# Soft-MoE kernel on one core: second expert product in four column groups, weight loads at the end of attention in a listed order

## The chip, the cores and the metric

One core of one Trainium2 chip runs the whole program. The metric is device time in microseconds (us). Runs of the kernel before: 588.32, 585.62 and 587.15 us, median 587.15. The profiled execution took 587.28 us; the trace spans 585.0 us of it, so 2.3 us lie around the trace.

## The reference, cut to what matters

Three layers, all in float32. The change lies in the second and in the way from the first to it.

```python
x = attention(q, k, v, cap)            # batch 4, 12 heads, 448 rows, 64 each -> [1792, 768]
logits = x @ phi                       # [1792, 32]: 8 experts with 4 slots each
d = softmax(logits, axis=0)            # over the tokens
slot_input = (d.T @ x).reshape(8, 4, 768)
for e in range(8):
    h = np.maximum(slot_input[e] @ w1[e], 0.0)     # w1[e] is [768, 1024]
    slot_out[e] = h @ w2[e]                        # w2[e] is [1024, 768]
x = softmax(logits, axis=1) @ slot_out.reshape(32, 768)
out = mlp(x, w_in, w_out, alpha)       # 768 -> 2048 -> 768
```

The expert weights are 8 x 6 MB. They are read once; each is multiplied with a few rows only.

## The kernel before, in words

**Attention** (`attention`, L243) runs over 24 pairs of heads, four chunks of keys a pair, in the order `CHUNKS = (0, 3, 1, 2)` (L53). `qk` makes a chunk's scores and their exponentials `p`; two steps later `pv` multiplies them with the values (`o`), GpSimd adds `p` of the chunks into `acc`, and `row_sums` multiplies `acc` with `hot` (`rs`); for the last pair also `p` of its last two chunks (`rs<-p`).

**Attention's room.** Attention's SBUF pools lie one after another (L248 to L263). Bytes per partition, counted from the first: `nat0` 0 to 4096, `nat1` to 8192, `stk0` to 15872, `vn0` to 17664, `acc0` to 21248, `stk1` to 28928, the four buffers of `pt` (a full chunk's `p`, 3584 bytes each) to 32512, 36096, 39680 and 43264, the two of `ptt` (chunk 3) to 46848, `vn1` to 48640, `acc1` to 52224, then constants, `xn` and others. Even pairs use `nat0`, `stk0`, `vn0`, `acc0`, odd ones the others. The framework deals the four `pt` buffers in a fixed round: first, fourth, third, second. In the compiled program of before the last full chunks therefore lie so: pair 22's chunk 2 in the first buffer, pair 23's chunk 0 in the fourth, its chunk 1 in the third, its chunk 2 in the second.

**Weights.** `loads` (a list made ahead of time) names every weight load in the order of its use: for each expert two halves of w1 and two of w2, 1.5 MB each; the first half of `w_out` stands before expert 7. `load_next` (L130) takes the next into the first free slot. All these transfers are issued by SyncE (SP), whose instructions run in order: one that waits holds up all behind it. Ten loads go into ten slots of their own during attention. The eleventh slot holds the conversion buffer `cvbuf` of `w_in` until its last converted piece is stored to a scratch tensor in HBM (`store_w_in`, L714, SP); that function then issues the eleventh load (two transfers, L172). Seven more slots (`xtra`, 12288 bytes each) lie over attention's room from byte 0. `load_free` at L1351 fills them, by `load_part` (L119): 3072-byte pieces of a w2 half (384 KB, four of them), 4096-byte pieces of a w1 half (512 KB, three). `in_turn` (L98) keeps all of these in one order. A piece waits for the last use of every attention tile that it overlaps. Later loads wait for slots that the experts give back (`done_with`).

**Experts** (`experts`, L858). For each expert: `h`, 6 steps of K in four column groups of 256 that run side by side in the array's column quarters (L869); ReLU on ScalarE (L880); two transposes (L885); a copy by VectorE (L886); then `y` (L893), 8 steps of K in three column groups of 256:

```python
yacc[32 * g:32 * g + 32, :256],
hT[:, kk % 2, kk // 2, :],
wv[kk % 4][:, 256 * g:256 * g + 256],
```

Each float32 product stands in the trace as two records, so a step of `y` has six. `y` accumulates over all experts. The slots' rows of `h` and `y` are 32 partitions.

**After the experts**, `gather` (L907) copies `y` out of PSUM (`ysb`), turns it with two transposes (`yt`), and copies it to `so`; `mlp` follows with `aps` (L930), which reads the first `w_in` load. `warm` products (L812) fill short waits of TensorE.

Of the kernel before, what the change touches and what calls it, by code (L numbers as in the profile page):

```python
# [8 lines left out]
F32 = mybir.dt.float32  # L9
# [15 lines left out]
def tile_attention_soft_moe_mlp(ctx, tc, q, k, v, cap, phi, w1, w2, w_in, w_out, alpha, out):  # L25
    nc = tc.nc
# [24 lines left out]
    LAG = 2  # L51

    CHUNKS = (0, 3, 1, 2)  # L53
    LOADS = (4, 6, 8, 10, 12, 14, 16, 18, 19, 20, 21, 22)

    EH = 5
# [37 lines left out]
    nload = [0]  # L94
    issued = [None]
    half = []

    def in_turn(ins):  # L98
        if xslots:
            if issued[0] is not None:  # L100
                tc.add_manual_dep(ins.ins, issued[0].ins.name, NOSYNC, reason="loads in the order of their use")
            issued[0] = ins

    def may_load():
        if nload[0] == len(loads):
# [13 lines left out]
    def load_part(kind, e, i, c, t, after=None):  # L119
        if kind == "w2":  # L120
            src = w2_rows(e, i)[:, c // 2, c % 2]
        else:
            src = w1_rows(e, i)[:, c]
        ins = nc.sync.dma_start(out=t, in_=src)
        in_turn(ins)
        if after is not None:
            tc.add_manual_dep(ins.ins, after.ins.name, NOSYNC, reason="prefetch pace")
        return t

    def load_next(after=None):  # L130
        slot_no = may_load()
        free.remove(slot_no)
        kind, e, i = loads[nload[0]]
        nload[0] += 1
        if slot_no >= NA:

            ts = where.setdefault((kind, e, i), [])
            n = 3 if kind == "w1" else 4
            for c in range(len(ts), n):
                t = xslots[0].tile([128, SLOT // n], F32, tag=f"slot{slot_no}_{c}", name="w")  # L140
                ts.append(load_part(kind, e, i, c, t))
            return
        if kind == "w1":
            t = slot(slot_no, [128, 3, FE])
            src = w1_rows(e, i)
        elif kind == "w2":
            t = slot(slot_no, [128, 4, DM])
            src = w2_rows(e, i)
        elif kind == "wi":
            t = slot(slot_no, [128, KD, 512])  # L150
            src = w_in32[i].rearrange("(k p) f -> p k f", p=128)
        else:
            t = slot(slot_no, [128, 2, DM, 2], U32)
            src = w_out[256 * i:256 * i + 256].rearrange("(k p) f t -> p k f t", p=128)
        if kind == "w1":
            parts = [(t, src)]
        elif kind == "w2":
            parts = [(t[:, 2 * j:2 * j + 2], src[:, j]) for j in range(2)]
        else:
            parts = [(t[:, c], src[:, c]) for c in range(t.shape[1])]  # L160
        if kind == "wo" and i == 0:

            half.append(parts.pop())
        elif kind == "wi" and i == 0:
            parts = [
                (t[:, ks, fs], src[:, ks, fs])
                for fs in (slice(0, 256), slice(256, 512))
                for ks in (slice(0, 3), slice(3, 6))
            ]
            parts[2:2] = half  # L170
        for dst, part in parts:
            ins = nc.sync.dma_start(out=dst, in_=part)  # L172
            in_turn(ins)
            if after is not None:
                tc.add_manual_dep(ins.ins, after.ins.name, NOSYNC, reason="prefetch pace")
        if kind == "w1":
            t = [t[:, c] for c in range(3)]
        elif kind == "w2":
            t = [t[:, c] for c in range(4)]
        where[kind, e, i] = t  # L180
        held[kind, e, i] = slot_no
# [61 lines left out]
    def attention():  # L243
        with ExitStack() as pools:
            def pool(name, bufs=1, **kw):
                return pools.enter_context(tc.tile_pool(name=name, bufs=bufs, **kw))
# [4 lines left out]
            v_0 = pool("vn0")  # L251
            acc_0 = pool("acc0")
            stk_1 = pool("stk1")
            pt_p = pool("pt", 4)
            ptt_p = pool("ptt", 2)
            v_1 = pool("vn1")
# [9 lines left out]
            ps_o = pool("ps_o", space=PSUM)  # L266

            nat_p, stk_p, v_p, acc_p = (nat_0, nat_1), (stk_0, stk_1), (v_0, v_1), (acc_0, acc_1)
            stackI = ac_p.tile([128, 128], F32, name="stackI")
            sel = ac0_p.tile([128, GP, 2, 2, 64], F32R, name="sel")  # L270
            hot = ac0_p.tile([128, 64], F32, name="hot")
# [441 lines left out]

            def store_w_in(i):  # L714
                fb, kk = divmod(i, KD)
                nc.sync.dma_start(out=w_in32[fb, kk * 128:(kk + 1) * 128, :], in_=cout.pop(i))
                load_w_in(i + 2)
                if i == ncv - 1:
                    free.append(NA - 1)
                    load_next()  # L720

            def run_bg():
                while bg and min(bg) <= now[0]:
# [78 lines left out]
    def tail():  # L802
# [50 lines left out]
                )  # L853
            nc.vector.tensor_copy(out=cstk[:, b * S:(b + 1) * S], in_=ps)

        G3 = DM // 256

        def experts(which, small, ps_w, yacc, cstk=None):  # L858
            for e in which:
                if e == E - 1:  # L860
                    to_single(0)
                    split_wo(0)
                hT = small[:, 0:256].rearrange("p (u j s) -> p u j s", u=2, j=4)
                nc.gpsimd.memset(hT, 0.0)
                h1 = ps_w.tile([128, 512], F32, tag="w", name="h1")[:, :256]
                for kk in range(KD):
                    wv = where["w1", e, kk // 3]
                    for j in range(4):
                        nc.tensor.matmul(  # L869
                            h1[32 * j:32 * j + 32, :],  # L870
                            slotT[:, kk, :],
                            wv[kk % 3][:, 256 * j:256 * j + 256],
                            start=(kk == 0),
                            stop=(kk == KD - 1),
                            tile_position=(0, 32 * j),
                        )
                done_with("w1", e, 0)
                done_with("w1", e, 1)
                rl = small[:, 256:512]
                nc.scalar.activation(  # L880
                    out=rl.rearrange("q (u p) -> q p u", u=2), in_=h1.rearrange("q (p u) -> q p u", u=2), func=AF.Relu
                )
                tp = ps_w.tile([128, 512], F32, tag="w", name="tp")[:, :256]
                for u in range(2):
                    nc.tensor.transpose(tp[:, 128 * u:128 * u + 128], rl[:, 128 * u:128 * u + 128], ident)  # L885
                nc.vector.tensor_copy(  # L886
                    out=hT[:, :, :, SPE * e:SPE * e + SPE],
                    in_=tp.rearrange("p (u j s) -> p u j s", u=2, j=4)[:, :, :, SPE * e:SPE * e + SPE],
                )
                for kk in range(KE):  # L890
                    wv = where["w2", e, kk // 4]
                    for g in range(G3):
                        pe[0] = nc.tensor.matmul(  # L893
                            yacc[32 * g:32 * g + 32, :256],
                            hT[:, kk % 2, kk // 2, :],
                            wv[kk % 4][:, 256 * g:256 * g + 256],
                            start=(e == 0 and kk == 0),
                            stop=(e == E - 1 and kk == KE - 1),
                            tile_position=(0, 32 * g),
                        )  # L900
                done_with("w2", e, 0)
                done_with("w2", e, 1)
                if EH <= e < EH + B // 2:
                    for b in (2 * (e - EH), 2 * (e - EH) + 1):
                        build_c(b, ps_w, cstk)

        def gather(ps_w, yacc, so):  # L907
            warm = ps_c.tile([128, 512], F32, tag="c", name="warm")
            idle(2, warm)
            ysb = unit(7, F32, "ysb")[:32 * G3, :256]  # L910
            nc.vector.tensor_copy(out=ysb, in_=yacc[:32 * G3, :256])
            yt = ps_w.tile([128, 512], F32, tag="w", name="yt")[:, :64 * G3]
            for u in range(2):
                pe[0] = nc.tensor.transpose(
                    yt[:, 32 * G3 * u:32 * G3 * (u + 1)], ysb[:, 128 * u:128 * u + 128], ident[:32 * G3, :32 * G3]
                )
            idle(3, warm)
            for r in range(2):
                dst = so[:, :, r, :].rearrange("p (g u) s -> p u g s", u=2)
                src = yt.rearrange("p (u g s) -> p u g s", u=2, g=G3)  # L920
                nc.vector.tensor_copy(out=dst, in_=src)

        def mlp(ps_w, ps_c, so, cstk, a_stk, gr, gs, ob, more):
# [415 lines left out]
        with (  # L1339
# [4 lines left out]
            with (  # L1344
# [3 lines left out]
                small = ex2_p.tile([128, 512], F32, name="small")  # L1348
                xslots.append(xt_p)
                free.extend(range(NA, NA + NX))  # L1350
                load_free()  # L1351
                experts(range(EH), small, ps_w, yacc)
            with (
                tc.tile_pool(name="r2", bufs=1, reuse_waits="tile") as r2_p,
# [48 lines left out]
```

## Time and profile before

| what | us |
|---|---|
| median of three runs | 587.15 |
| profiled execution | 587.28 |
| span of its trace | 585.0 |
| TensorE busy | 553.1 (95% of the span) |
| VectorE busy | 435.1 (74%) |
| ScalarE busy | 377.6 (65%) |
| share of the chain that ended last: TensorE, DMA | 71%, 14% |
| of which: load of expert weights | 9% |

How to read it: attention lasts to about 261 us, the experts to 327 us, the MLP from there to the end. TensorE is busy nearly always, but a stage can still be held by something else: in the page's 40 slices (14.6 us each) the transfers move 347 to 419 GB/s in slices 17 to 25 (234 to 366 us), which hold the experts' stage, and 53 GB/s in slice 16, just ahead. The chain of waits tells which of the two ended last.

### The profile page before, as it was taken

The numbers are of one execution on the slowest core, as the hardware profiler recorded it, in microseconds if no ns is written. First come the engines' busy times: TensorE is split into PE (matmuls) and PEld (weight loads), VectorE is DVE, ScalarE is ACT, GpSimd is POOL, SyncE is SP. The second block draws the span as 40 slices with busy tenths as digits, with TensorE's granted clock in tenths as the row PEclk, the third lists the DMA queues.
The fourth block names the chain that finished last, engine by engine and source line by source line (L and its number), as shares of the span: only waits on it lengthen the run. The fifth ranks groups of instructions, "written<-read, shape, count | busy, mean of one in ns | idle before, by whom it ended". The sixth has DMA issues, their size and how long they took to land.

```text
span 585.0 us, 10832 instructions
## 1 busy us (share of the span) xinstructions
PE 553.1 (95%) x4030; PEld 384.7 (66%) x4030; DVE 435.1 (74%) x834; ACT 377.6 (65%) x617; POOL 173.9 (30%) x158
## 2 busy tenths in 40 slices
PE   5999999999999999998888799999999999999996
PEld 4444444445444545464445577878888999999996
DVE  3878777796999768460023489999999979797974
ACT  3999999898889788530011266854777755555551
POOL 0789788676785755500000000000000000000000
PEclk9999999999999999999999999999999999999999
DMA  7668789987787971999999999200120101010101
GB/s 174 155 141 251 230 263 269 266 255 200 225 256 214 326 229 53 350 347 418 416 417 419 390 404 414 111 1 1 55 55 1 55 1 54 2 55 0 55 2 54
DMA packets 83460, 110.92 MB, mean 190 GB/s; under 512 B 55376, under 2 KB 63312, under 8 KB 81872
## 3 DMA queue, kind: packets, MB, share of 16 engines
q1 hardware_dynamic: 81168, 109.28, 55.3%
q10 hardware_dynamic: 2240, 0.95, 0.6%
q8 instruction: 32, 0.52, 0.4%
q14 instruction: 20, 0.16, 0.1%
HBM read 98.41 MB, written 11.80 MB: 188 GB/s over the span
## 4 chain that ended last, share of the span: by engine, by line
PE 71%; DMA 14%; ACT 8%; DVE 5%; issue 2%; SPq 1%; ACTq 0%
PE o L295 10%; DMA w<-in_moe_w_dram 9%; PE s L295 8%; PE P L1229 7%; PE P L1227 7%; PE P L1228 7%; PE oc L1002 6%; PE oc L1008 6%; PE oc L1009 6%; DMA v<-in_v_dram 3%; ACT p L398 2%; PE aps L930 2%; ACT p L397 2%; PE nx L295 2%; PE rs L295 2%
## 5 line engine op out<-in xcount | busy, mean ns | idle before, releaser
L295 PE MATMUL o<-p,v 128*64 128x448 f32 (+1 forms) x384 | 93.3, 564 | 5.8 <-ACT xu L423 3.7
L397 ACT ACTIVATE p<-s 128x896 f32<-128x896 f32 x96 | 78.7, 821 | 21.1 <-PE s L295 18.0
L398 ACT ACTIVATE p<-p,cap 128x896 f32<-128x896 f32 x96 | 90.9, 949 | 2.3
L414 POOL TENSOR_TENSOR acc<-p 128x448 f32<-128x448 f32 x48 | 62.1, 1313 | 55.6 <-ACT p L398 55.6
L1008 PE MATMUL oc<-wsp,gr 128*128 128x512 f32 (+1 forms) x192 | 65.3, 341 | 0.0
L1009 PE MATMUL oc<-wsp,gr 128*128 128x512 f32 (+1 forms) x192 | 64.1, 337 | 0.0
L1002 PE MATMUL oc<-wsp,gr 128*128 128x512 f32 (+1 forms) x192 | 62.6, 343 | 0.0
L295 PEld LDWEIGHTS s<-qh,kh 64*128 64x128 f32 (+1 forms) x168 | 18.1, 185 | 66.5 <-issue 25.6
L1218 ACT ACTIVATE gr<-gs 128x384 fp32r<-128x384 f32 (+1 forms) x64 | 36.7, 576 | 32.8 <-DVE gs L1202 26.9
L417 POOL TENSOR_TENSOR acc<-acc,p 64x448 f32<-64x448 f32 x46 | 55.4, 1204 | 1.7
L421 POOL TENSOR_TENSOR acc<-acc,p 128x448 f32<-128x448 f32 x46 | 53.5, 1183 | 1.8
L1219 DVE TENSOR_TENSOR gr<-gs,gr 128x384 fp32r<-128x384 f32 x64 | 39.2, 620 | 17.4 <-ACT gr L1218 17.4
L295 PE MATMUL s<-qh,kh 64*128 64x448 f32 (+1 forms) x168 | 45.8, 473 | 0.0
L1227 PE MATMUL P<-wsp,gr 128*128 128x384 f32 x128 | 42.9, 335 | 0.0
L1229 PE MATMUL P<-wsp,gr 128*128 128x384 f32 x128 | 42.8, 334 | 0.0
L1228 PE MATMUL P<-wsp,gr 128*128 128x384 f32 x128 | 42.8, 334 | 0.0
L1002 PEld LDWEIGHTS oc<-wsp,gr 128*128 128x128 f32 x192 | 36.6, 192 | 5.6 <-ACT wsp L837 0.8
L1008 PEld LDWEIGHTS oc<-wsp,gr 128*128 128x128 f32 x192 | 36.8, 191 | 5.2 <-DVE wx L205 0.4
L1009 PEld LDWEIGHTS oc<-wsp,gr 128*128 128x128 f32 x192 | 36.3, 189 | 4.4 <-issue 0.4
L295 PEld LDWEIGHTS o<-p,v 128*64 128x64 f32 (+1 forms) x384 | 19.0, 134 | 30.3 <-ACT xu L423 12.3
L295 PE MATMUL s<-ql,kh 64*128 64x448 f32 (+1 forms) x168 | 35.5, 366 | 1.0 <-DVE ql L377 1.0
L295 PE MATMUL s<-qh,kl 64*128 64x448 f32 (+1 forms) x168 | 35.5, 365 | 0.0
(237 smaller groups left out, 1227.3 us busy)
## 6 DMA issues: line engine op xcount, KB each, us to landing
w<-in_moe_w_dram SPq DMA_DIRECT2D x26, 768.0 KB, 12.4
w<-in_moe_w_dram SPq DMA_DIRECT2D x12, 1536.0 KB, 12.2
cvbuf<-in_moe_w_in_dram SPq DMA_DIRECT2D x24, 512.0 KB, 5.4
w<-in_moe_w_out_dram SPq DMA_DIRECT2D x16, 768.0 KB, 11.1
w_in<-cvbuf SPq DMA_DIRECT2D x24, 256.0 KB, 2.8
w<-in_moe_w_dram SPq DMA_DIRECT2D x12, 512.0 KB, 7.4
q<-in_q_dram SPq DMA_DIRECT2D x44, 112.0 KB, 3.6
k<-in_k_dram SPq DMA_DIRECT2D x48, 96.0 KB, 4.8
```

Source lines behind the costliest of these rows:

```text
L295: ins = nc.tensor.matmul(*a, **kw)
L397: nc.scalar.activation(out=pe, in_=ps[:, :n, :S], func=AF.Tanh)
L398: nc.scalar.activation(out=pe, in_=pe, func=AF.Exp, scale=cap_sb)
L414: nc.gpsimd.tensor_add(out=a[:, u, :], in0=pt[i, 0][:, u, :], in1=pe[:, u, :])
L417: nc.gpsimd.tensor_add(out=a[r, u, :], in0=a[r, u, :], in1=pt[i, JK][r, 0, :])
L421: nc.gpsimd.tensor_add(out=a[:, u, :], in0=a[:, u, :], in1=pe[:, u, :])
L1002: ins = nc.tensor.matmul(o, gh[:, ts], wo_h[f][:, cols], start=(f == 0 and not second), stop=False)
L1008: nc.tensor.matmul(o, gh[:, ts], wo_l[f][:, cols], start=False, stop=False)
L1009: nc.tensor.matmul(o, gl[:, ts], wo_h[f][:, cols], start=False, stop=(f == KF - 1 and not more))
L1227: nc.tensor.matmul(o, hi[:, i], bh, start=(p == 0), stop=False)
L1228: nc.tensor.matmul(o, hi[:, i], bl, start=False, stop=False)
L1229: nc.tensor.matmul(o, lo[:, i], bh, start=False, stop=(p == 7))
```

## The change

- `y` takes four column groups of 192 in place of three of 256. A group's 192 columns are three runs of 64 that stand 256 apart in the weight row. A step has eight records in place of six.
- `gather` copies 128 x 192 in place of 96 x 256; six products with parts of the identity (64 columns each, in the two column halves) take the place of the two transposes; the copies to `so` keep their size.
- The last w2 half of expert 7 is read by three transfers (768, 384, 384 KB) in place of two of 768 KB.
- `store_w_in` no longer issues the eleventh load. `load_free` collects the transfers of that load and of the seven slots, and they are issued in the order `FIRST`, the others behind. They are numbered: 0 and 1 the eleventh load; 2 to 5 the first `xtra` slot (bytes 0 to 12288); 6, 7, 8 the second (to 24576); 9, 10, 11 the third (to 36864); 12 to 15 the fourth (to 49152); 16 to 19 the fifth; 20 to 25 the last two. Before, their order is 0 to 25.
- The last store of `w_in` is put behind transfers 2 and 3.
- A pool `edge` of 256 bytes stands between `stk1` and `pt`: the `pt` buffers then end at 32768, 36352, 39936 and 43520. So piece 10 (28672 to 32768) meets the first buffer alone, piece 12 (36864 to 39936) the third alone, 13 the fourth, 11 the second and third, 14 the fourth and `ptt`. Without the 256 bytes, piece 10 also meets 256 bytes of the second, and 12 of the fourth.

```diff
+    FIRST = [2, 3, 4, 5, 0, 1, 6, 12, 7, 8, 9, 13, 14, 10]
...
+    def transfer(dst, src, after=None):
+        if collected:
+            collected.append((dst, src))
+            return
+        ins = nc.sync.dma_start(out=dst, in_=src)
+        in_turn(ins)
...
+            if e == E - 1 and i == 1:
+                parts[1:] = [(t[:, 2 + u], src[:, 1, u]) for u in range(2)]
...
             stk_1 = pool("stk1")
+            edge = pool("edge")
             pt_p = pool("pt", 4)
...
                 if i == ncv - 1:
                     free.append(NA - 1)
-                    load_next()
...
-        G3 = DM // 256
+        G4 = DM // 192
...
-                    for g in range(G3):
+                    cols = wv[kk % 4].rearrange("p (u g c) -> p g u c", u=3, g=G4)
+                    for g in range(G4):
                         pe[0] = nc.tensor.matmul(
-                            yacc[32 * g:32 * g + 32, :256],
+                            yacc[32 * g:32 * g + 32, :192],
                             hT[:, kk % 2, kk // 2, :],
-                            wv[kk % 4][:, 256 * g:256 * g + 256],
+                            cols[:, g],
...
+            odd = ident.rearrange("p (k r s) -> p r k s", r=2, s=32)
+            for u in range(3):
+                for r in range(2):
+                    pe[0] = nc.tensor.matmul(
+                        yt[64 * r:64 * r + 64, 64 * u:64 * u + 64], ysb[:, 64 * u:64 * u + 64], odd[:, r],
+                        start=True, stop=True, tile_position=(0, 64 * r),
+                    )
...
+                collected.append(None)
                 load_free()
+                todo = collected[1:]
+                collected.clear()
+                first = FIRST
+                for n in first + [n for n in range(len(todo)) if n not in first]:
+                    transfer(*todo[n])
+                    if n == first[1]:
+                        tc.add_manual_dep(
+                            last_store[0].ins, issued[0].ins.name, NOSYNC, reason="room that is free sooner"
+                        )
```

## Rows read from the trace of the kernel before

**Rows 1.** Chain of waits, experts' stage: start us, us, what

```profile
271.02 17.63 DMA w<-in_moe_w_dram
...
307.39 18.76 DMA w<-in_moe_w_dram
...
326.20 1.06 PE y L893 x12
```

**Rows 2.** Timeline of TensorE, experts: start us, us, [idle before <-releaser]

```profile
261.64 2.80 PE L869 MATMUL h<-w,slotT 128*32 128x256 f32 x48
...
284.97 2.94 PE L869 MATMUL h<-w,slotT 128*32 128x256 f32 x45
...
289.49 3.44 PE L893 MATMUL y<-w,small 128*32 128x256 f32 x45 [0.35 <-DVE small L886]
...
324.24 1.06 PE L893 MATMUL y<-w,small 128*32 128x256 f32 x12 [0.23 <-DMA w<-in_moe_w_dram]
326.20 1.06 PE L893 MATMUL y<-w,small 128*32 128x256 f32 x12 [0.90 <-DMA w<-in_moe_w_dram]
```

**Rows 3.** Stretches: us, PE PEld DVE ACT POOL busy, PEclk, DMA share, GB/s

```profile
231.00:234.00 3.00, 3.00 (x38) 1.42 (x34) 2.51 (x5) 2.85 (x4) 1.38 (x1) 1.00 0.21 64
...
241.00:244.00 3.00, 2.95 (x24) 1.03 (x22) 0.38 (x1) 2.87 (x4) 0.62 (x1) 1.00 1.04 418
...
249.50:251.30 1.80, 1.80 (x20) 1.00 (x16) 1.76 (x2) 1.27 (x3) 0.00 (x0) 1.00 0.27 55
...
271.00:290.00 19.00, 16.29 (x227) 8.44 (x222) 0.58 (x3) 1.83 (x3) 0.62 (x2) 1.00 1.02 419
```

**Rows 4.** Timeline of SP's DMA issues around attention's end: start us, us

```profile
233.09 0.33 SPq L716 DMA_DIRECT2D w_in<-cvbuf  x1
...
235.17 0.81 SPq L172 DMA_DIRECT2D w<-in_moe_w_dram  x2
...
240.43 0.33 SPq L124 DMA_DIRECT2D w<-in_moe_w_dram  x1
...
243.66 1.28 SPq L124 DMA_DIRECT2D w<-in_moe_w_dram  x3
...
250.05 0.33 SPq L124 DMA_DIRECT2D w<-in_moe_w_dram  x1
...
264.23 0.33 SPq L124 DMA_DIRECT2D w<-in_moe_w_dram  x1
```

**Rows 5.** The issue at 250.05 us: KB, us from issue to landing

```profile
w<-in_moe_w_dram SPq DMA_DIRECT2D x1, 512.0 KB, 3.8
```

**Rows 6.** Timelines of TensorE and GpSimd: last uses of the `pt` buffers

```profile
239.42 0.97 PE L295 MATMUL o<-p,v 128*64 128x448 f32 x4
...
245.70 0.97 PE L295 MATMUL o<-p,v 128*64 128x448 f32 x4
...
249.00 0.97 PE L295 MATMUL o<-p,v 128*64 128x448 f32 x4
...
243.38 2.28 POOL L414 TENSOR_TENSOR acc<-p 128x448 f32<-128x448 f32 x2 [3.57 <-ACT p L398]
```

**Rows 7.** Chain of waits: four column groups of 128 columns, 6 steps of eight records

```profile
256.82 1.51 PE ss L295 x48
```

**Rows 8.** Timelines of VectorE and TensorE: `gather`

```profile
327.32 0.42 DVE L911 COPY ysb<-y 96x256 f32<-96x256 f32 x1 [5.29 <-PE y L893]
...
327.79 0.39 PE L914 MATMUL yt<-ident,ysb 96*128 96x96 f32 x2
```

**Rows 9.** Two stretches (columns as in rows 3), and the chain inside and behind the second

```profile
331.00:334.70 3.70, 1.73 (x12) 1.19 (x10) 2.92 (x7) 1.65 (x4) 0.00 (x0) 1.00 1.03 404
...
335.50:338.90 3.40, 3.40 (x20) 2.69 (x16) 3.34 (x7) 2.63 (x6) 0.00 (x0) 0.50 1.06 394
...
338.05 0.43 PE oc L1002
...
339.19 0.23 PE oc L1008
```

More of the change, by code (lines that the diff above doesn't have):

```diff
@@ L96, in tile_attention_soft_moe_mlp @@
     half = []
+    collected, last_store = [], []
     def in_turn(ins):
@@ L102, in in_turn @@
             issued[0] = ins
+    def transfer(dst, src, after=None):
[4 more added lines that the diff above has]
+        in_turn(ins)
+        if after is not None:
+            tc.add_manual_dep(ins.ins, after.ins.name, NOSYNC, reason="prefetch pace")
     def may_load():
@@ L123, in load_part @@
             src = w1_rows(e, i)[:, c]
[L124 to L127, printed above, removed]
+        transfer(t, src, after)
         return t
@@ L171, in load_next @@
         for dst, part in parts:
[L172 to L175, printed above, removed]
+            transfer(dst, part, after)
         if kind == "w1":
@@ L268, in attention @@
             nat_p, stk_p, v_p, acc_p = (nat_0, nat_1), (stk_0, stk_1), (v_0, v_1), (acc_0, acc_1)
+            edge.tile([128, 64], F32, name="edge")
             stackI = ac_p.tile([128, 128], F32, name="stackI")
@@ L715, in store_w_in @@
                 fb, kk = divmod(i, KD)
-                nc.sync.dma_start(out=w_in32[fb, kk * 128:(kk + 1) * 128, :], in_=cout.pop(i))
+                last_store[:] = [nc.sync.dma_start(out=w_in32[fb, kk * 128:(kk + 1) * 128, :], in_=cout.pop(i))]
                 load_w_in(i + 2)
@@ L909, in gather @@
             idle(2, warm)
[L910 to L916, printed above, removed]
+            ysb = unit(7, F32, "ysb")[:, :192]
+            nc.vector.tensor_copy(out=ysb, in_=yacc[:, :192])
+            yt = ps_w.tile([128, 512], F32, tag="w", name="yt")[:, :192]
+            odd = ident.rearrange("p (k r s) -> p r k s", r=2, s=32)
[5 more added lines that the diff above has]
+                    )
             idle(3, warm)
             for r in range(2):
-                dst = so[:, :, r, :].rearrange("p (g u) s -> p u g s", u=2)
-                src = yt.rearrange("p (u g s) -> p u g s", u=2, g=G3)
+                dst = so[:, :, r, :]
+                src = yt.rearrange("p (k s) -> p k s", s=32)
                 nc.vector.tensor_copy(out=dst, in_=src)
```

## The prediction, made before the changed kernel was run

> **What bounds the kernel now.** I read the chain of waits first. Through the experts it is made of weight loads, the last of them issued at 307.39 and landed at 326.15, and then one piece of `y` [rows 1]. TensorE's own timeline shows that it is nearly level with them: it works from 261.64 and waits for loads only at the end, 0.23 and 0.90 us [rows 2]. So two things of nearly equal length end this stage at 327.26: TensorE's 64.5 us of expert work, and a stream of loads. Taking 6.9 us off the first alone could show only about 1 us, for the stream ends at 326.15 whatever TensorE does.
>
> The stretches say when the stream can be shortened: not inside (418 and 419 GB/s, in 384 KB pieces and in larger ones alike), but where it stands: before 236 (64 GB/s between 231 and 234) and from 249.5 to 251.3 (55 GB/s) [rows 3]. SP's issues tell why: the eleventh load goes out at 235.17, behind the store at 233.09; pieces 6 (240.43), 7 (243.66), 10 (250.05) and 25 (264.23) wait for room [rows 4].
>
> **The change part by part.**
>
> *`y` in four groups.* From the two rows of `y`, 45 records in 3.44 and 12 in 1.06, a step of six records takes (3.44 - 1.06) / 5.5 = 0.433 us, and a start and end add 0.19 [rows 2]. With 192 columns a group in place of 256 the step becomes 0.325 if it goes by a group's columns. More records could bound it: eight in four groups have gone by in 1.51 / 6 = 0.25 [rows 7], below 0.325, so I take 0.325. What runs of 64 columns cost is shown nowhere: between nothing and a doubled step (a rival). Saved: 64 steps x 0.108 = 6.9 us of TensorE, 57.6 left, which would end at 319.3. The loads are later, so on the path this is worth only the last step's part, below.
>
> *The head of the stream.* Pieces 2 and 3 lie over `nat0` and `nat1`, which the transposes of pair 23 release near 228; they can go out behind pair 23's values at about 231. The store at 233.09 then stands behind two issues of some 0.4 us each, and its data behind 768 KB, 1.9 us; what waits for it is the eleventh load (pieces 0 and 1), and 4 and 5 (1.9 us of transfer) cover that. An issue into an empty stream lands 3.8 us later with 512 KB [rows 5], of which 1.25 are transfer at 418 GB/s and 2.5 fixed. Piece 6 waits for the `o` products of pair 22's last chunk, to 240.39 [rows 6], as now. So at that point the new stream has done all of 0 to 6 by about 244, and the old one was some 3 us behind.
>
> *The listed order.* Behind 6 comes 12. It meets the third `pt` buffer, which by the dealing of before holds pair 23's chunk 1: GpSimd reads it to 243.38 + 2.28 = 245.66, and the `o` products to 245.70 + 0.97 = 246.67 [rows 6]. So SP stands from about 241 to 246.75. Queued behind are 7, 8 and 9 (free at 243.66 now [rows 4]), 13, 14 and 10 (by the padding clear of the second buffer, held to 249.97), and all later loads. The stream runs dry near 244. From 12 on it carries the eight pieces 12 to 19 and the eleven pieces 7 to 11 and 20 to 25: 8 x 384 + 11 x 512 = 8704 KB, 21.3 us. Before, from 250.05, the eight and eight others: 7168 KB, 17.6 us. 246.75 + 21.3 = 268.05 against 250.05 + 17.6 = 267.65: the stream ends 0.4 **later**, though it began 4 us earlier. The hole of before is filled and another opened of the same size. Piece 11 (249.97) and 25 (264.23) are then no longer waited for.
>
> *The end.* All later loads are one stream with over 10 us of issues ahead (18.8 us from issue to landing at the last [rows 1]), so 0.4 is carried to the end. The split of the last transfer into 384 KB adds one issue, hidden by that lead, and I put 0.05 on it. What follows the last landing is one step, 0.325 + 0.19 = 0.52, in place of 1.06. The last landing moves to 326.6, `y` ends at 327.2: 0.1 earlier.
>
> Pieces of 384 KB move at the rate of larger ones here [rows 3]. The Trainium skill, "DMA: Bandwidth & Descriptors", section "Rules for kernel authors", asks for 1 MiB or more a transfer for full bandwidth, and section "Anatomy of one DMA" gives a fixed cost of about 2.0 us for one (on GpSimd's path); an estimate by that page, unhidden, would put 2 us on the split. The trace disagrees: the fixed part is hidden while others are in flight.
>
> *`gather`.* `ysb` has 192 columns in place of 256: 0.42 becomes 0.32 [rows 8]. Six products of 64 columns for two transposes of 0.39 together: from equal, if pairs run side by side, to 0.84 (three times 0.28). Near the lower end, as the four groups of `h` run side by side (6 steps in 2.80 [rows 2]): +0.14. Sum +0.04, and no change on the stage behind: its first load follows the last of the experts' by the same transfers.
>
> *Sum:* 0.4 + 0.05 - 0.54 + 0.04 = -0.05 on the profiled execution's 587.28, so 587.2; the median of the runs is 587.15, the same within 0.15.
>
> **The rivals.**
>
> *A. Piece 12 is free early.* If the changed program deals the `pt` buffers so that the third holds pair 22's chunk 2 (free at 240.39), then 12 follows 6 at once, 7 goes out at 243.66, and from there 8320 KB, 20.4 us, are left: 264.1, bounded by piece 25's issue, 264.23 + 1.25 = 265.5, against 267.65. That is a gain of 2.2, or of 3.6 were 25 free; I take 3.4, since a stream a few per cent slower than 418 GB/s reaches piece 25 after it is free. With -0.54 and +0.1: 587.3 - 3.8 = 583.5. TensorE's 319.3 still lies ahead, so both parts would pay. For it: piece 10's wait to 249.97 in the trace fits this dealing too, since it only says that the last chunk lies in the first two buffers. Against: the dealing is a fixed round in the program of before, and the change adds no tile to it.
>
> *B. The clock, the slower side.* TensorE will be done with expert 6 near 311 (7.8 us an expert now, three from 261.64 to 284.97 [rows 2], 6.9 then, and the transposes for the later stage) and then stand until expert 7's w1 lands (326.6 minus 7.5 us for w2 and 3.75 for a w1 half: 315.3), and again until 319. In the trace it was busy 1.73 of 3.70 us before 335, and then the granted clock was 0.50 (1.2 GHz) for 3.4 us, a product taking 0.43 in place of 0.23 [rows 9]. If the low stretch covers only the first half of `h`, nothing shows, the loads being later. It decides from where it lasts beyond about 321: then the second half of `h`, transposes and `y` at half speed end near 328.8, +1.6, and `gather` and `aps` lose up to 1.8 more: 588.8 to 590.6. By the Trainium skill, "TensorE: Matmul & The Clock Gate", section "Why this matters for your kernels", idle gaps between bursts of products bring the throttled clock back; the trace agrees at 335. Under A the waits are shorter and this is less likely.
>
> *C. Runs of 64 columns are slow.* With a doubled step (0.65) TensorE would need 64.5 + 13.9 = 78.4 us and end at 340: 600. It decides from a step of 0.45, where TensorE's slack of 327.2 - 319.3 = 7.9 us over 64 steps is gone. No row shows such reads, and none excludes a cost.
>
> *D. In between:* 12 waits, but less (1 to 2 us), or the holes close otherwise: 584.5 to 586.
>
> **How the numbers follow.** What a measurement here tells from no change is 0.5%, 2.9 us: 584.2 and 590.1 are the bounds. Forecast 0.44 (own range 586.2 to 588.3), A 0.32, B 0.13, D 0.07, C 0.04. Faster: the larger part of A, 0.27, and 0.03 for the low stretch at 335 falling away on top of D. Slower: C and some of B, 0.08. Same: 0.62. The range reaches into A and B: 582.7 to 589.3; outside lie C, the upper end of B and 0.1 of A, below 582.7.
>
> **What would show it.** Right: SP's issue of 12 just behind the `o` products that end near 246.7, with 7, 8, 9 within 1.5 us behind it; a stretch near 244 to 248 with few GB/s; 250 without one; last landing within 0.7 us of 326.6; a `y` step of 0.32 to 0.33, TensorE's waits for loads in expert 7 at 5 us or more. Wrong: 12 issued near 241 (A), the last landing near 323; `y` steps above 0.44 (C); a granted clock of 0.50 between 314 and 330 with the end of `y` over 1 us behind the last landing (B).

## The result, and the profile after

| | before | after |
|---|---|---|
| median of the runs, first measurement (4 and 4 runs), us | 586.43 | 590.46 |
| ratio, 95% interval | | 1.006 (1.0040 to 1.0081) |
| median, measured again beside the experiments (31 and 8), us | 586.16 | 590.5 |
| ratio, 95% interval | | 1.0076 (1.0047 to 1.0106) |
| profiled execution, us | 587.28 | 590.82 |
| mean granted clock of TensorE | 0.997 | 0.989 |

The change makes the kernel 4 us slower. 590.46 lies above the predicted range (582.7 to 589.3). In the profile after, TensorE's clock is at 0.50 (1.2 GHz in place of 2.4) three times for 3.4 us each, from 261.9, 316.6 and 384.8 us; in the profile before it is so once, from 335.5 (the last 5 us of each trace left out).

**The loads.** SP's issues and the stretches, profile after (columns as in [rows 4] and [rows 3]):

```profile
231.58 1.06 SPq L110 DMA_DIRECT2D w<-in_moe_w_dram  x2
233.56 0.33 SPq L725 DMA_DIRECT2D w_in<-cvbuf  x1
...
240.90 0.33 SPq L110 DMA_DIRECT2D w<-in_moe_w_dram  x1
...
247.31 1.75 SPq L110 DMA_DIRECT2D w<-in_moe_w_dram  x4
...
263.61 0.33 SPq L110 DMA_DIRECT2D w<-in_moe_w_dram  x1
```

```profile
231.00:234.00 3.00, 3.00 (x34) 1.55 (x31) 2.77 (x6) 2.89 (x4) 0.91 (x1) 1.00 0.63 175
241.00:244.00 3.00, 2.94 (x26) 1.17 (x24) 0.00 (x0) 2.87 (x5) 0.16 (x1) 1.00 0.91 318
244.00:248.00 4.00, 4.00 (x55) 1.39 (x54) 3.48 (x6) 1.61 (x2) 2.11 (x2) 1.00 0.12 43
249.50:251.30 1.80, 1.80 (x17) 0.74 (x17) 1.80 (x3) 0.81 (x2) 0.00 (x0) 1.00 1.09 406
271.00:290.00 19.00, 16.30 (x300) 9.62 (x296) 0.57 (x3) 1.83 (x3) 0.94 (x3) 1.00 1.01 417
```

Piece 6 goes out at 240.90 and nothing behind it until 247.31, when 12, 7, 8 and 9 follow one another. From 244 to 248 the stream moves 43 GB/s; the hole of before at 249.5 (55 GB/s) is filled (406). At 231 the stream starts earlier (175 against 64 GB/s). Piece 25 is the issue at 263.61 (264.23 before).

**The experts' end.** TensorE's timeline, profile after (columns as in [rows 2]):

```profile
311.87 2.16 PE L902 MATMUL y<-w,small 128*32 128x192 f32 x48
317.14 2.79 PE L877 MATMUL h<-w,slotT 128*32 128x256 f32 x24 [3.10 <-DMA w<-in_moe_w_dram]
...
326.44 1.53 PE L902 MATMUL y<-w,small 128*32 128x192 f32 x24 [1.06 <-DMA w<-in_moe_w_dram]
328.45 0.53 PE L902 MATMUL y<-w,small 128*32 128x192 f32 x8 [0.48 <-DMA w<-in_moe_w_dram]
...
329.55 0.57 PE L925 MATMUL yt<-ident,ysb 128*64 128x64 f32 x12
...
330.92 1.53 PE L942 MATMUL aps<-w,so 128*64 128x128 f32 x24
```

The last landing is at 328.40 (before 326.15), `y` ends at 328.98 (before 327.26): 1.7 us late, of which 0.5 were there before the experts (`h` begins at 262.19 against 261.64 [rows 2]). The span grew by 4.0, so over 2 us must come from behind. There the source was touched in `gather` alone.

**The second block of layers** (`mlp`). Its products on TensorE are `aps` (the slots times `w_in`), `hps` (the hidden values of the tokens, one of 16 blocks at a time) and `oc` (times `w_out`); VectorE converts a block of `w_out` into `wx`, and ScalarE and VectorE copy that into `wsp`, which `oc` reads. The same stretch of 18 us in both traces (columns as in [rows 3]), before and then after:

```profile
372.00:390.00 18.00, 18.00 (x104) 14.05 (x103) 17.77 (x27) 11.40 (x19) 0.00 (x0) 1.00 0.00 1
```

```profile
372.00:390.00 18.00, 15.94 (x78) 12.59 (x78) 18.00 (x28) 12.13 (x19) 0.00 (x0) 0.91 0.01 3
```

Before, TensorE is busy all of it at full clock. After, it stands for 2.06 us and then runs at a mean clock of 0.91, which is 3.4 us at 0.50 (half of that, 1.7 us, lost). TensorE's wait, after (TensorE's timeline):

```profile
381.31 0.39 PE L974 MATMUL hps<-cstk,a_stk 128*128 128x512 f32 x1
383.60 1.50 PE L1014 MATMUL oc<-wsp,gr 128*128 128x512 f32 x6 [1.90 <-ACT wsp L845]
...
387.10 0.63 PE L1020 MATMUL oc<-wsp,gr 128*128 128x512 f32 x1
```

It waits for ScalarE's copy `wsp` of `w_out`'s block 8. ScalarE's timeline shows one half of why; after first, then before:

```profile
378.94 0.90 ACT L201 ACTIVATE wf<-w 128x768 f32<-128x768 f32 x1
381.74 0.60 ACT L980 ACTIVATE gs<-hps 128x512 f32<-128x512 f32 x1 [1.89 <-PE hps L974]
382.23 0.59 ACT L981 ACTIVATE gs<-hps 128x512 f32<-128x512 f32 x1
382.71 1.58 ACT L845 ACTIVATE wsp<-wx 128x768 fp32r<-128x768 f32 x2
```

```profile
378.42 1.73 ACT L194 ACTIVATE wf<-w 128x768 f32<-128x768 f32 x2
380.16 1.58 ACT L837 ACTIVATE wsp<-wx 128x768 fp32r<-128x768 f32 x2
381.64 0.61 ACT L978 ACTIVATE gr<-gs 128x512 fp32r<-128x512 f32 x1
382.16 0.58 ACT L968 ACTIVATE gs<-hps 128x512 f32<-128x512 f32 x1
```

Before, the two copies (blocks 8 and 9) come ahead of the two ReLUs of hidden block 10. After, the ReLUs come first. They wait 1.89 us for `hps`, which TensorE issues only at 381.31, and start at 381.74.

The copies could not have gone much sooner, though. VectorE finishes the input of the first one at 381.65 (380.70 + 0.95), 0.09 us before the ReLUs start. VectorE's timeline, after; then the same operation in the changed kernel without the split (run 3 below), whose `mlp` has the order of before, and the copies there:

```profile
380.70 0.95 DVE L212 SCALAR_TENSOR_TENSOR wx<-w,wx 128x768 uint32<-128x768 uint32 x1
```

```profile
379.33 0.95 DVE L210 SCALAR_TENSOR_TENSOR wx<-w,wx 128x768 uint32<-128x768 uint32 x1
...
380.32 1.58 ACT L843 ACTIVATE wsp<-wx 128x768 fp32r<-128x768 f32 x2
```

Counted from the end of `y` (328.98 and 328.68), TensorE issues this `hps` at 52.33 and 52.32, the same. The input is ready at 52.67 after and at 51.60 in the old order, 1.07 us later; the copies start at 53.73 and 51.64, so that the two ReLUs ahead of them add about 1.0. Each half makes some 1 us of the loss.

The same source lines run in another order: the framework puts all instructions of a program in order, and a change upstream moved that order (by what reckoning, no run shows). In `mlp` 116 of 1410 places on TensorE, 73 of 304 on ScalarE and 77 of 458 on VectorE differ.

### The profile page after: what moved, and what is told of

It reads as the page before. It is cut to its first block, busy times and chain, and to the rows that moved or that the text cites. A ratio compares the mean times of both kernels' runs of the same rounds, so it can differ in the third digit from the quotient of the medians.

```text
span 589.0 us, 11103 instructions
## 1 busy us (share of the span) xinstructions
PE 551.6 (94%) x4168; PEld 385.0 (65%) x4168; DVE 440.4 (75%) x834; ACT 378.0 (64%) x617; POOL 175.5 (30%) x158
## 4 chain that ended last, share of the span: by engine, by line
PE 63%; DMA 19%; ACT 8%; DVE 6%; issue 2%; SPq 1%; ACTq 0%
PE o L304 10%; DMA w<-in_moe_w_dram 9%; PE s L304 9%; PE P L1241 6%; PE P L1240 6%; PE P L1239 6%; DMA w<-in_moe_w_out_dram 6%; PE oc L1020 4%; PE oc L1014 4%; PE oc L1021 4%; PE nx L304 2%; PE rs L304 2%; ACT p L407 2%; ACT p L406 2%; PE tr L304 1%
## 5 line engine op out<-in xcount | busy, mean ns | idle before, releaser
L423 POOL TENSOR_TENSOR acc<-p 128x448 f32<-128x448 f32 x48 | 62.6, 1324 | 53.8 <-ACT p L407 53.7
L1021 PE MATMUL oc<-wsp,gr 128*128 128x512 f32 (+1 forms) x192 | 64.9, 341 | 0.0
```

The source lines that it names most:

```text
L423: nc.gpsimd.tensor_add(out=a[:, u, :], in0=pt[i, 0][:, u, :], in1=pe[:, u, :])
L1021: nc.tensor.matmul(o, gl[:, ts], wo_h[f][:, cols], start=False, stop=(f == KF - 1 and not more))
```

## The experiments

My theory was this order; the rivals were the later loads and the granted clock. Single executions of the kernel before spread over 4 to 6.5 us in a round of runs, so ratios are to runs of the kernel before on the same chip at the same time.

**1. The order of before in the changed kernel, and the new order in the kernel before.** Every instruction of `mlp` on the three engines is chained to its predecessor in the wanted order (through a wrapper around the engines, so that traces of these kernels name its line, L45):

```diff
+                for name, notes in nc._tape.items():
+                    turn = written_out(ORDER_OF[name])
...
+                    for n, m in zip(turn, turn[1:]):
+                        tc.add_manual_dep(notes[m].ins, notes[n].ins.name, NOSYNC, reason="order of the other kernel")
```

> The changed kernel with one thing put back: the second block of layers (from a_block to the last store) issues its instructions on TensorE, ScalarE and VectorE in the order in which the kernel before issued them (116 of 1410 places on TensorE differ, 73 of 304 on ScalarE, 77 of 458 on VectorE; no instruction is added or left out). Theory 'order': the 3.6 us that the changed kernel lost between 337 and 387 us come from that other order, so the time is 590.5 - 3.6 = 586.9 us, there is no wait of TensorE on ScalarE's wsp near 383 and no low clock at 384.8, while the expert stage keeps its later last landing (about 2 us after the one of before). Rival 'late loads': the same 3.6 us come from weights that land later, whatever the order: 590.5 us, with the same wait on wsp or a DMA wait in its place. Rival 'clock': the low clock at 384.8 is chance: it returns in some executions and not in others, and the time lies between, 588 to 590.5 us.

> The kernel before with one thing of the changed kernel's: the order of the instructions of the second block of layers on TensorE, ScalarE and VectorE. Loads, the y product and the gather are those of before. Theory 'order': 586.4 + 3 to 3.6 = 589.4 to 590.0 us, with a wait of TensorE on ScalarE's wsp of some 2 us near 380 and a stretch at the lower clock behind it. Rival 'late loads': no change, 586.4 us. Rival 'clock': between, 586.4 to 588.

Measured: the changed kernel with the old order 587.96 us, ratio 1.0020 (1.0004 to 1.0036); the kernel before with the new order 588.73 us, 1.0025 (1.0008 to 1.0042). So 0.4 to 0.56% (2.3 to 3.3 us) of the loss goes with the order, and some 1.5 us (0.5 to 2.5) come with it into the kernel before. That is less than the 3.6 us that I expected of either: taking the order out gives back most of the loss, putting it in makes less than half of it. The time of the first run, at the edge of the 588 to 590.5 us of the rival 'clock', doesn't exclude it; the wait does better, for it stands in every profile with the new order, with a low clock behind it or without. TensorE's row in the kernel before with the new order:

```profile
383.61 1.75 PE L45 MATMUL oc<-wsp,gr 128*128 128x512 f32 x5 [1.90 <-ACT wsp L45]
```

The wait is the same 1.90 us with the loads of before. The later loads aren't needed for it.

**2. One edge.** If one place makes the wait, one edge must undo it:

```diff
-            nc.scalar.activation(out=both[:, 0], in_=t, func=AF.Copy)
+            splits[f] = nc.scalar.activation(out=both[:, 0], in_=t, func=AF.Copy)
...
+                    if (tb, f) == (0, 10):
+                        for ins in relus:
+                            tc.add_manual_dep(ins.ins, splits[9].ins.name, NOSYNC, reason="behind the split")
```

> The changed kernel itself, timed in the same rounds as the three runs beside it, since single runs of one kernel spread over some 4 us (584.9 to 589.7 in 35 runs of the kernel before). All theories: 589 to 590.5 us, and the wait of TensorE on wsp near 383.

> The changed kernel with one ordering edge added on ScalarE and nothing else: the two relus of hidden unit 10 in the second block of layers are not issued before the copy that makes the upper half of w_out's block 9. In the changed kernel these relus (381.74 us) stand ahead of the copies for blocks 8 and 9 (382.71) and wait 1.89 us there for TensorE's hps; TensorE then waits 1.90 us for the copy of block 8 (383.60) and runs at the lower clock from 384.8 to 388.2. Theory 'one place in the order': the wait of 2.1 us and the low clock behind it (3.4 us at half speed, 1.7 us) both go: 3.5 us less than the changed kernel in the same rounds, 586 to 587 us. Rival 'the whole order': other places of the 73 that differ on ScalarE or the 116 on TensorE carry the loss: less than 1 us is gained, 589 to 590 us.

Measured: the changed kernel 590.5 us, with the edge 588.24 us (1.0034, 1.0016 to 1.0051): 2.3 us less, not 3.5, between the theory's 586 to 587 and the rival's 589 to 590. TensorE and ScalarE show what is left:

```profile
383.14 1.42 PE L1020 MATMUL oc<-wsp,gr 128*128 128x512 f32 x6 [0.88 <-ACT wsp L846]
```

```profile
382.25 1.58 ACT L846 ACTIVATE wsp<-wx 128x768 fp32r<-128x768 f32 x2 [1.83 <-DVE wx L212]
```

The copies are ahead of the ReLUs now, but VectorE, whose order the edge leaves as it is, delivers their input at 382.21, so 0.88 us of the 1.90 stay. The edge takes out ScalarE's half of the wait, and the low clock behind it is gone from this profile. In the changed kernel's second profile the wait is there without a low clock behind it:

```profile
385.14 1.42 PE L1014 MATMUL oc<-wsp,gr 128*128 128x512 f32 x6 [1.91 <-ACT wsp L845]
```

**3. What moved the order.** In the programs as they are built, the list, the padding and the `y` product leave `mlp` in its old order; the split of the last w2 transfer alone moves it. The edit, taken from the changed kernel and, in the second run, put alone into the kernel before:

```diff
-            if e == E - 1 and i == 1:
-                parts[1:] = [(t[:, 2 + u], src[:, 1, u]) for u in range(2)]
```

> The changed kernel without the split of the last w2 transfer (one of 768 KB again in place of two of 384 KB); y in four groups, list and padding stay. Two lines of source less, and the second block of layers is then issued in the order of the kernel before on all three engines. Theory 'the split moves the order': no wait on wsp near 383 and no low clock behind it, 590.5 - 2.4 (what the old order gave) + 0.5 (a last step that waits for 768 KB in place of 384) = 588.0 to 588.6 us. Rival 'the split only halves the last landing's piece': 590.5 + 0 to 0.5 us.

> The kernel before with the split of the last w2 transfer alone (the two lines that the run beside it leaves out). Theory 'the split moves the order': the order of the second block of layers becomes nearly that of the changed kernel (9 of 304 places on ScalarE differ from it, 75 from the kernel before), the two relus of unit 10 stand ahead of the copies for blocks 8 and 9, TensorE waits about 2 us for wsp near 380, and the time is 1.8 to 3 us above the kernel before: 588 to 589 us. Rival 'the split is worth what it was meant for': half a piece less behind the last landing, 0.3 to 0.5 us below the kernel before.

Measured: without the split 588.93 us, 1.0027 (1.0011 to 1.0043); the kernel before with the split 587.81 us, 1.0023 (1.0006 to 1.0041), less than the 1.8 to 3 us that I expected of it. Two lines that touch one transfer of expert 7 cost the kernel before 1.4 us, 55 us behind their place. TensorE's row there:

```profile
381.45 1.42 PE L1004 MATMUL oc<-wsp,gr 128*128 128x512 f32 x6 [1.91 <-ACT wsp L839]
```

and the stretch in the changed kernel without the split, without the wait and at full clock:

```profile
372.00:390.00 18.00, 18.00 (x105) 14.09 (x105) 17.76 (x27) 11.38 (x19) 0.00 (x0) 1.00 0.01 2
```

**4. The blocked piece.** Pieces 10 and 12 change places:

```diff
-    FIRST = [2, 3, 4, 5, 0, 1, 6, 12, 7, 8, 9, 13, 14, 10]
+    FIRST = [2, 3, 4, 5, 0, 1, 6, 10, 7, 8, 9, 13, 12, 14]
```

> The changed kernel with pieces 10 and 12 of its list swapped (10 goes out eighth, 12 thirteenth), so that nothing stands before the piece that lies over the third pt buffer but pieces that are free by 245.7. The order in the second block of layers stays the changed kernel's. Both theories on the loads: SP issues 10, 7, 8 and 9 near 243 to 244.5 in place of 247.3 to 248.6, the hole of 245 to 248.5 us (35 GB/s) is filled but for piece 13 at 245.7 and 12 at 246.7, and the last landing comes about 3 us sooner than in the changed kernel (325.5 in place of 328.4). Theory 'order': what the second block of layers loses stays, so the time is 590.5 less what the y product's end moves, at most 3 us: 587.5 to 590.5. Rival 'late loads': the loads are back at or ahead of where they were before, so the whole loss goes: 583.5 to 586.5 us.

> The same edge and pieces 10 and 12 of the list swapped. The two losses lie one behind the other, so they should add: the swap alone took the changed kernel to 586.8 us; less the 3.5 us of the wait and the low clock, 583.3 us, 3 to 4 us ahead of the kernel before. Rival: the wait at 383 covers time that the sooner loads gain, so that only one of the two is kept: 585.5 to 586.8 us.

> Pieces 10 and 12 swapped, and the second block of layers in the order of the kernel before on all three engines. With the old order the changed kernel ran 588.0 us; the swap took 2 to 3 us off the y product's end. Theory: 585.0 to 586.0 us, with TensorE's low clock of 335 to 339 us back (14.0 us at a mean clock of 0.90 in the kernel before, 1.4 us lost), so above the run with the one edge. Rival: the old order is the better one throughout, 583.5 us or less.

> The changed kernel with pieces 10 and 12 swapped and without the split: what the change does if neither the blocked piece nor the new order is in it. Against the run with the swap and the old order written out (585.0 us, 1.2 below the kernel before) only the split is missing: +0.3 to 0.5, so 585.3 to 585.6 us. Theory of the sum: 590.5 - 2.4 (order) - 3.0 (loads sooner) + 0.5 = 585.6. Rival: the order written out costs or gives something by itself; then this run lies over 1 us from 585.3.

Measured: the swap alone 586.83 us (0.9996, 0.9981 to 1.0012), between the ranges of the two theories, so that it doesn't part them; with the edge 584.91 (0.9970, 0.9948 to 0.9991), between the 583.3 of the sum and the rival's 585.5; with the old order 585.01 (0.9973, 0.9954 to 0.9992), as expected; without the split 585.99 (0.9983, 0.9966 to 1.0001), 0.4 above what I expected. Each is 2.6 to 4.7 us below its sibling without the swap (differences of the ratios, 0.0044 to 0.0080, times 586.4), and two of them are ahead of the kernel before. The stretches with the swap and the edge:

```profile
241.00:244.00 3.00, 2.95 (x26) 1.32 (x24) 0.00 (x0) 2.87 (x5) 0.00 (x0) 1.00 1.00 408
244.00:248.00 4.00, 4.00 (x56) 1.41 (x48) 3.48 (x6) 1.92 (x3) 2.28 (x2) 1.00 0.82 249
```

249 GB/s in place of 43 from 244 to 248: behind piece 6, SP issues the next at 243.77 and not at 247.31.

**5. The `y` product.** Alone in the kernel before, and left out of the changed one (the product and its `gather` put back; the first lines of that edit):

```diff
-        G4 = DM // 192
+        G3 = DM // 256
```

> The kernel before with the second product in four column groups of 192 and its gather alone; loads, padding and the order in the second block of layers as before. The prediction's step: each product 2.8 in place of 3.44 to 3.8 us, hidden by the loads except in the last step (-0.54) and the gather (+0.04): 586.4 - 0.5 = 585.9 us. Theory 'order': nothing more, 585.5 to 586.4. Rival: the shorter product leaves TensorE waiting longer for loads and the clock falls in the stage behind, 587.5 to 588.5 us.

> The changed kernel's loads (list, padding, split) with the y product and the gather of the kernel before, and the second block of layers in the order of the kernel before. Against the changed kernel with the old order (588.0 us, 1.0 above the kernel before) only y differs: eight records of 192 columns a step against six of 256. The prediction's step: y counts only behind the last landing, 0.54 less 0.04, so this run is 0.5 us slower, 588.5 us. Rival: the shorter y makes TensorE stand longer and run at the lower clock at the stage's end, so that leaving it out gains: 586.5 to 587.5 us.

> The changed kernel without the split and with y and gather of the kernel before: the pair of the run that gave 588.9 us, only y differing, the order of the second block of layers as built and equal to the kernel before. Theory 'clock': no low clock before 330, y ends about 1.1 us behind the last landing: 586.3 to 587.3 us. Rival 'y is worth 0.5 us': 589.4 us.

> The changed kernel's list with 10 and 12 swapped and its padding, without the split, and with y and gather of the kernel before. Theory: with y in three groups TensorE has 64.5 us of expert work from 261.6 us on, so that y can't end before 326.1, however soon the loads land: 1.1 us ahead of the kernel before at most, 585.3 us, with no wait of TensorE for loads and no low clock before 330. Rival 'loads bound': y ends with the loads near 325, as with four groups, and without their low clock: 584 us.

Measured: `y` alone 587.39 us (1.0015, 0.9998 to 1.0031), not the 585.9 that I expected, and nearer the rival's 587.5 to 588.5; all but `y` in the old order 586.29 (0.9993, 0.9977 to 1.0009), and without the split 587.41 (1.0017, 0.9998 to 1.0037); all but `y`, with the swap and without the split, 585.6 (0.9996, 0.9971 to 1.0021). The three pairs with and without the new `y` (1.0020 and 0.9993, 1.0027 and 1.0017, 0.9983 and 0.9996) have overlapping intervals: `y` isn't worth the 0.5 us that I gave it, and whether it costs something with late loads isn't settled. Alone, its profile shows why no gain came: `y` ends 0.90 us behind the last landing in place of 1.11, and `gather` takes 0.26 more. In the run with the swap and the old `y`, TensorE never waits for loads from 300 us to the end of `y`, and the stage takes 64.3 us from `h` to the end of `y`: there TensorE is the bound, as expected.

The traces show a difference, though. The end of the experts in the changed kernel without the split, and in its pair with the old `y`:

```profile
315.53 2.79 PE L875 MATMUL h<-w,slotT 128*32 128x256 f32 x24 [4.08 <-DMA w<-in_moe_w_dram]
...
323.75 4.93 PE L900 MATMUL y<-w,small 128*32 128x192 f32 x64 [0.35 <-DVE small L892]
```

```profile
324.70 3.93 PE L899 MATMUL y<-w,small 128*32 128x256 f32 x48 [0.35 <-DVE small L892]
```

With four groups TensorE stands 4.08 us before expert 7, the granted clock then is 0.50 (1.2 GHz) from 314.5 to 328.2, and `y`, which needs 2.8 us at full clock, takes 4.93 and ends 1.64 us behind the last landing. With three groups the clock stays at full and `y` ends 1.11 behind it.

**6. Filling the waits.** Products whose results aren't used, ahead of each w1 half of expert 7 (16 and 3; with the swap 7 and 6):

```diff
+                    if last and kk in (0, 3):
+                        idle({0: 16, 3: 3}[kk], warm)
...
```

> The changed kernel without the split (588.9 us), with 16 products of 128 columns ahead of expert 7's first w1 half and 3 ahead of its second, where TensorE waited 4.08 and 0.82 us for loads; their results are not used. Such a product takes about 0.23 us, so 3.7 and 0.7 us of the waits are filled. Theory 'clock': the granted clock no longer falls to 0.50 at 315 to 329; the last eight steps of y take 2.8 instead of 4.9 us, y ends about 1.1 us behind the last landing (a piece of 768 KB) instead of 1.64, and gather's start is at full speed: 0.6 to 1.2 us less, 587.7 to 588.3. Rival 'not the clock': no change or, where a load comes sooner than the filling ends, up to 0.5 more: 588.9 to 589.4 us.

> Pieces 10 and 12 swapped, no split, 7 and 6 filling products in expert 7 (waits of 1.64 and 2.10 us there). Theory 'clock': the low clock of 318 to 324 goes, y follows the last landing by 1.0 in place of 1.15 us: 0.2 to 0.8 less than without filling, 585.2 to 585.8 us. Rival: nothing to gain, since the low clock there ended with the loads: 586.0 us.

Measured: 589.05 us (1.0050, 1.0026 to 1.0073), nothing gained; with the swap 584.49 (0.9973, 0.9947 to 0.9999), which is below the unfilled 585.99 and below the 585.2 to 585.8 expected, but with overlapping intervals. Without the swap the low clock left its place, and there is one later:

```profile
312.15 3.84 PE L818 MATMUL warm<-ident 128*128 128x128 f32 x32
316.65 1.50 PE L879 MATMUL h<-w,slotT 128*32 128x256 f32 x24 [0.67 <-DMA w<-in_moe_w_dram]
...
327.89 1.29 PE L910 MATMUL y<-w,small 128*32 128x192 f32 x16 [1.12 <-DMA w<-in_moe_w_dram]
329.12 1.22 PE L818 MATMUL warm<-ident 128*128 128x128 f32 x4
330.27 0.91 PE L933 MATMUL yt<-ident,ysb 128*64 128x64 f32 x12
```

`h` takes 1.50 in place of 2.79 us, but `warm` and `yt` now take 1.22 and 0.91 in place of 0.71 and 0.57: the clock is at 0.50 from 328.2 to 331.6 and once more from 338.4, near where the kernel before has its low clock. So the expectation of the theory 'clock' held up to the last landing and failed behind it. With the swap it held: the same stretch (columns as in [rows 3]) unfilled, then filled, whose profile has no low clock at all before the end of `mlp`:

```profile
318.00:325.00 7.00, 5.70 (x66) 2.81 (x62) 0.19 (x1) 0.61 (x1) 0.00 (x0) 0.51 1.03 397
```

```profile
318.00:325.00 7.00, 4.32 (x74) 2.13 (x74) 0.19 (x1) 0.61 (x1) 0.00 (x0) 1.00 1.02 398
```

**All runs in one table.** From the profiled execution of each: the last landing counted from the first `h` (this leaves attention's jitter out), the end of `y` counted from there, and the time from there to the last `oc`, us.

| kernel | order of `mlp` | landing - `h` | `y` end - landing | `oc` end - `y` end | ratio |
|---|---|---|---|---|---|
| before | old | 64.51 | 1.11 | 128.64 | 1 |
| `y` alone | old | 64.73 | 0.90 | 128.95 | 1.0015 |
| before, new order | new | 65.25 | 1.11 | 130.70 | 1.0025 |
| before and split | near new | 65.17 | 0.68 | 128.72 | 1.0023 |
| after, first profile | new | 66.21 | 0.58 | 130.90 | 1.0060 |
| after, second profile | new | 66.01 | 1.75 | 129.42 | 1.0076 |
| after, old order | old | 66.06 | 1.04 | 128.90 | 1.0020 |
| after, one edge | new, edge | 66.51 | 1.19 | 128.27 | 1.0034 |
| after, no split | old | 65.89 | 1.64 | 127.38 | 1.0027 |
| after, no split, filled | old | 65.92 | 1.34 | 130.02 | 1.0050 |
| after, old `y`, old order | old | 65.53 | 0.68 | 127.11 | 0.9993 |
| after, old `y`, no split | old | 65.80 | 1.11 | 127.11 | 1.0017 |
| swap | new | 62.64 | 0.58 | 130.92 | 0.9996 |
| swap, edge | new, edge | 63.12 | 0.57 | 128.30 | 0.9970 |
| swap, old order | old | 63.06 | 0.58 | 128.92 | 0.9973 |
| swap, no split | old | 63.10 | 1.15 | 127.37 | 0.9983 |
| swap, no split, filled | old | 63.95 | 0.90 | 127.37 | 0.9973 |
| swap, old `y`, no split | old | 63.15 | 1.11 | 127.12 | 0.9996 |

The three columns are the three terms. Loads: 64.5 to 65.3 with the list of before, 65.5 to 66.5 with the changed one, 62.6 to 64.0 with the swap. The end of `y` at full clock: with the split 0.58 (four groups) and 0.68 (three), without it 0.90 and 1.11; 1.0 to 1.75 where a low clock reaches the landing. The stage behind: 127.1 in the old order with the old `gather`, 127.4 with the new; with a low clock from 335 to 338 on, 128.6 to 129.0 (130.0 where one at 328 goes before it); in the new order 130.7 to 130.9 with the low clock near 384, and 129.4 without (128.7 in the near-new order with the old `gather`); with the edge 128.3.

## Why the prediction was wrong

- **The step that failed:** *`gather`*, "and no change on the stage behind: its first load follows the last of the experts' by the same transfers". That reason looks at the loads alone. The stage behind changed its order and cost 2.0 us of waiting (129.42 against 127.38 at equal clock, both with the new `gather`; 1.6 with the split in the kernel before, 128.72 against 127.11). A low clock follows the wait in three of the five profiles with it, for 1.5 us more; the kernel before has a low clock of the same size elsewhere, at 335 [rows 9]. Runs 1 to 3 show the order's cost in both directions. No rival held it either: I asked what each edit costs where it stands, and never which instructions the framework would put elsewhere because of it.
- **Last-transfer split:** I costed it at 0.05. Where it stands it gives what a smaller last piece should (`y` ends 0.58 in place of 0.90 behind the landing), and through the order it costs more than that: leaving these two lines out gave 1.9 to 2.9 us back.
- **The listed order:** mechanism right. Piece 12 was issued at 247.31 (forecast 246.75, and attention ran 0.5 late), 7, 8 and 9 within 1.3 us behind it, the stretch 244 to 248 at 43 GB/s. The size was off: the loads end 1.1 us later (mean of the table's eight rows with the changed list 66.0, of the four with the list of before 64.9), not 0.4 + 0.05. The two profiles say where a large part of it arises. In the 30 us ahead of the first `h` the stream moves 284 GB/s for 20 us and 392 for 10 before, 262 and 401 after: 0.35 MB behind, 0.8 us at 417 GB/s. From there to 62 us on the two move alike (417 and 416). So this lag is made around the holes and carried through the experts. In this pair the last landing itself comes 1.7 us later; where the other 0.9 arises wasn't followed. Rival A was wrong about which buffer lies there; its price is borne out: with a free piece in 12's place the loads end 2.8 us sooner than in the changed kernel (mean of the six rows 63.2), and the time falls by 2.6 to 4.7 us (A's 583.5 lies 3.7 under the forecast). Against the kernel before, the best of these runs gains 1.8 us (0.9970).
- **`y` in four groups:** the step is (2.16 - 0.19) / 6 = 0.33 us, as forecast (0.325); runs of 64 columns cost nothing that shows, so C is out. The last step ended 0.58 behind the landing (0.52 forecast), 0.53 less than before; the split alone brings 0.43 of that (0.68 with three groups), four groups the other 0.10.
- **`gather`:** +0.26, not +0.04: 1.94 us from the end of `y` to `aps` against 1.68; the twelve records of `yt` take 0.57, and the six products start one after the other, most of them 0.06 us apart, not in pairs.
- **Rival B** came about in part. The granted clock fell to 0.50 before expert 7 in all five unfilled profiles with the changed list and four groups; in four of them it lasted to between 327.9 and 329.8 and `y` ended 1.04 to 1.75 us behind the landing. I gave it a chance of 0.13 and a price of 1.6 us or more; it came much oftener, and cost 0.5 to 1.2 us.

The sum for the first profile, by the table and attention: 0.55 (`h` starts later) + 1.70 (landing) - 0.53 (`y`) + 2.26 (stage behind, of which 0.26 is `gather`) + 0.06 (what follows `oc`) = 4.04, the growth of the span.

The Trainium skill, "TensorE: Matmul & The Clock Gate", section "Why this matters for your kernels", warns that idle gaps between bursts of products bring the throttled clock back; the gaps that it names are longer than the one here, and than those of 1.19 and 0.82 us ahead of the low clock at 335 before. In the trace the clock is at 0.50 from 384.8, behind a wait of 1.90 us, and the second profile shows the same wait without it. No profile without this wait has a low clock near 384, so the wait looks like a cause, but not a sure one.

What stays open: how much of the time the low clock before expert 7 costs by itself, since filling the waits took it away in one pair of runs and not in the other; and what decides whether the low clock at 335 comes.

## What to carry to other kernels

Where a framework orders the instructions, an edit can cost where it isn't: compare the order in which each engine's instructions are issued, through the end of the program, before believing that a stage "isn't touched". An in-order queue is worth reading for who stands behind a waiting instruction, and also for when what stands there was ready: on SP ready pieces stood behind one that waited, on ScalarE the copies lost 1.0 us behind two ReLUs and as much by an input that came late. Fix the order by an edge where it matters, check which half of the wait it takes away, and put behind the free pieces the one that is late.

## What the runs showed of the hardware that was not expected

- Filling the waits with unused products took TensorE's low clock out of 314.5 to 328.2 us, but in that profile it came at 328.2 and at 338.4, and nothing was gained (1.0050 against 1.0027, with overlapping intervals). With the swap, the filled profile has none where the unfilled one has it from 318.2 to 325.0. One profile of each doesn't say that it moves.
- With the same products and the same wait (1.90 and 1.91 us) the clock fell behind it in one execution of the changed kernel and not in the next.
